# A token-and-channel mixing kernel behind random-feature attention: a new job order, new slots and new engines for the same operations

## The chip, the cores and the metric

The kernel runs on one core of a Trainium2 chip. The core has five engines with a queue each: PE (TensorE, matrix products), DVE (VectorE), ACT (ScalarE), POOL (GpSimd) and SP (which here only issues DMAs). PE writes its results to eight banks of PSUM; DVE and ACT read them from there and write to the on-chip memory SBUF. The metric is the device time of one execution in microseconds, the median of several runs; less is better.

## The reference

Eight batches, 8 heads, 576 positions, head size 64, 128 random features. Attention without softmax gives `x`; a mixing over the positions and one over the channels follow, each with a skip connection.

```
def phi(x):                       # q and k, scaled by 64 ** -0.25
    proj = einsum('bhsd,md->bhsm', x, omega)
    h = proj - sum(x * x) / 2
    return exp(h - max(h)) / sqrt(128)
kv  = einsum('bhsm,bhsd->bhmd', k_p, v);   z = sum_s k_p
x   = (q_p @ kv) / (q_p @ z + 1e-06)       # to (8, 576, 512)
u   = x + (relu(x^T @ w_tok1) @ w_tok2)^T  # 576 -> 256 -> 576
out = u + relu(u @ w_ch1) @ w_ch2          # 512 -> 1536 -> 512
```

## The kernel before

Each batch is worked as 512 main positions, in four blocks of 128, and 64 tail positions. The tails of two batches fill the 128 rows of a block, and those of all eight make a ninth "batch" for the channel mixing. So there are nine channel-mixing stages, 0 to 8; the text calls them stage 0 to 8.

The program is a list of 1211 jobs. Each job has an engine and a function that issues its instructions. The lists at the top of the file say everything about time: `ORDER` is the order in which the functions are called, and so the order of each engine's own queue; a negative number in it is a filler matmul on zeros, into the bank that it names. `SLOT` gives, in that order, the bank or ring slot that a job's new buffer takes. `MOVED` puts single jobs on another engine than the usual one. Within an engine nothing overtakes; between engines semaphores hold a job until its operands are there and its bank is free.

The jobs of one batch, by the names in the code, with their lines:

- `kp`, `qp`, `kt`, `qt` (L650 to L669): features of k and q; ACT takes their exponentials (L515).
- `km` (DVE, L681) the maximum of a key's features, `vs` (POOL, L687) the scaled v, `kv` (PE, L702), `kv_out` its copy, `num` (PE, L735), `num_out` (DVE, L744) the division, which gives `x`.
- `t1`, `t2` (PE, L778 and L791) the token mixing, with `t1_tail` (L771); its relu goes to ACT or DVE; `uadd` (DVE, L794) adds `x`. `htt` (PE, L845) is the same for the tails of two batches, with two adds on DVE (L851). Then a DMA transposes `u`; in batch 0 PE does that, with copies `ut_out`.
- `c1` (PE, L967), 12 jobs of four matmuls, each with a relu on ACT or DVE (L290, L292).
- The second product of the channel mixing. In stage 0 it is plain (`c2`, L1001). In stages 1 to 8 `channel_out_fast` (L858) does it in seven products in place of eight (L917, 12 matmuls each), with sums of the relu's blocks and differences of the weights. The products have the numbers k0 to k6. k0 and k1 read the relu's blocks as they are, and so does k6, behind the first sum; k2 reads the third sum, k3 the first, k4 the second and k5 the fourth. The four sums (L879) are made in two halves of 128 x 768, each half in a chain of four. A product is added to the output by a read on DVE (L906). Stage 8 does each product in two halves.

In the job lists, an ACT or DVE job that the planner may move asks `engine(...)` for its place. The sums do that too:

```
def tt(eng, **kw):
    (nc.gpsimd if eng == "POOL" else nc.vector).tensor_tensor(**kw)
...
    e_sum = engine("DVE")
    def go(...):
        o, a, b = what()
        tt(e_sum, out=o[:, part], in0=a[:, part], in1=b[:, part], op=op)
    job = add(e_sum, 0.5, key + KEYS["S"] + 0.1 * g + 0.01 * k, go, deps=[*need, *prev], take=[("S", c)])
```

Of the kernel before, what the change touches and what calls it, by code (L numbers as in the profile page):

```python
# [81 lines left out]
]  # L82
SLOT = (
    "0001203450670100531642027046313724005203716031213170242506371243501030126450300623741115037622415010"
    "3157143302010163207240531170360711422336140014632220751302761220105427113005401216030201704522131743"
    "5632010231741610520432015370243105072320714330625120712006304015123156124230220105611334112101502001"
# [985 lines left out]
```

## Time and profile before

| what | value |
|---|---|
| median of three runs | 283.71 us (283.15 to 284.58) |
| span of the profiled execution, from its first to its last instruction | 281.1 us |
| the profiled execution's own time | not listed beside its span; the runs above stand for it |
| PE busy | 270.3 us, 96% |
| DVE busy | 222.4 us, 79% |
| ACT busy | 138.6 us, 49% |
| POOL busy | 92.0 us, 33% |
| instructions | 6278 |

The page divides the span into 40 slices and writes the busy tenths of each engine. The table of stretches gives for any window each engine's busy microseconds and its count of instructions, then the granted PE clock, the busy share of the DMA engines and the GB/s. The chain of waits follows the work that ended last back through what released it. In the timeline a row has its start, its length, the engine, the line, what it writes and reads, its shape and the number of instructions merged into it; in brackets stands how long the engine was idle before and who ended that. The length of a matmul is modelled with its way through the array, so a row of several is a little longer than the number times the pitch.

### The profile page before, as it was taken

The page shows a single profiled execution, that of the slowest core. Times are in us where ns is not written, and L with a number is a line of the kernel's source. Part 1 is how long each engine was busy: PE and PEld are TensorE (multiplying, and loading weights), DVE is VectorE, ACT ScalarE, POOL GpSimd, SP SyncE. Part 2 cuts the span into 40 slices and gives each one's busy share as a digit, 9 for nine tenths or more (in the row PEclk, how much of TensorE's full clock was granted, in tenths as well). Part 3 has the DMA queues.
Part 4 walks back from the last instruction along what each step waited for, and adds up shares of the span by engine and source line. Part 5 has one row for each costly group of instructions (what it writes and reads, how often), then busy time and mean ns, then how long its engine had stood idle before and what let it go on. Part 6 is the DMA issues. An engine that isn't in the chain of part 4 may idle for free.

```text
span 281.1 us, 6278 instructions
## 1 busy us (share of the span) xinstructions
PE 270.3 (96%) x2526; PEld 167.6 (60%) x2526; DVE 222.4 (79%) x462; ACT 138.6 (49%) x288; POOL 92.0 (33%) x116
## 2 busy tenths in 40 slices
PE   6899999999999999999999999999999999999993
PEld 2547546443657755665667647755676467446782
DVE  2589828499999899996997999977995893565992
ACT  1498994049676418743758445734753510031200
POOL 8574994007510872048008710510033000000001
PEclk9999999999999999999999999999999999999999
DMA  6999999999998999997979993960151304030125
GB/s 161 194 189 161 157 169 213 178 191 202 179 218 184 148 172 186 181 198 104 212 178 185 241 135 101 161 156 2 76 97 59 111 0 96 0 149 2 75 90 135
DMA packets 80524, 39.66 MB, mean 141 GB/s; under 512 B 63984, under 2 KB 76016, under 8 KB 80304
## 3 DMA queue, kind: packets, MB, share of 16 engines
q0 software_dynamic: 31744, 17.74, 44.1%
q1 hardware_dynamic: 46832, 15.77, 29.1%
q10 hardware_dynamic: 1920, 5.77, 5.4%
q8 instruction: 19, 0.31, 0.4%
q14 instruction: 9, 0.07, 0.1%
HBM read 35.95 MB, written 16.52 MB: 187 GB/s over the span
## 4 chain that ended last, share of the span: by engine, by line
PE 89%; DVE 3%; DMA 2%; ACT 2%; issue 0%; SPq 0%; DVEq 0%
PE bank L967 32%; PE bank L917 26%; PE bank L791 5%; PE bank L778 5%; PE bank L1001 4%; PE bank L735 3%; PE bank L657 3%; PE bank L702 3%; DMA wc<-in_k_dram 2%; PE bank L669 2%; ACT kp L515 1%; PE bank L845 1%; PE bank L817 1%; PE bank L737 1%; PE bank L771 1%; DVE T L448 1%
## 5 line engine op out<-in xcount | busy, mean ns | idle before, releaser
L967 PE MATMUL bank<-uT,wc 128*128 128x512 f16 x376 | 89.6, 379 | 0.5 <-DVE r L292 0.4
L290 ACT ACTIVATE r<-bank 128x512 f16<-128x512 f32 (+1 forms) x86 | 47.7, 601 | 82.7 <-PE bank L967 61.5
L295 POOL TENSOR_TENSOR vs<-v,vs 128x512 f16<-128x512 f16 x32 | 34.2, 1072 | 94.4 <-DVE vs L683 51.3
L967 PEld LDWEIGHTS <-wc 128*128 128x128 f16 x424 | 38.8, 98 | 38.8 <-issue 1.6
L917 PEld LDWEIGHTS <-r 128*128 128x128 f16 x384 | 36.8, 98 | 8.2 <-issue 1.1
L515 ACT ACTIVATE kp<-bank 128x512 f16<-128x512 f32 x64 | 36.7, 618 | 8.9 <-PE bank L657 7.1
L515 ACT ACTIVATE qp<-bank 128x512 f16<-128x512 f32 x64 | 36.7, 614 | 8.8 <-PE bank L669 5.8
L681 DVE TENSOR_REDUCE km<-kp 128x8 f16<-128x1024 f16 x32 | 38.7, 1208 | 1.2 <-ACT kp L515 1.1
L292 DVE TENSOR_SCALAR r<-bank 128x512 f16<-128x512 f32 (+1 forms) x40 | 26.3, 670 | 15.7 <-PE bank L967 11.3
L745 DVE TENSOR_TENSOR x<-bank,rc 128x320 f16<-128x320 f32 x62 | 30.5, 492 | 2.1
L917 PEld LDWEIGHTS <-S 128*128 128x128 f16 x288 | 28.1, 98 | 5.8 <-issue 0.3
L906 DVE TENSOR_TENSOR o<-u,bank 128x512 f32<-128x512 f16 x28 | 19.0, 679 | 6.2 <-PE bank L917 5.8
L917 PE MATMUL bank<-T,r 128*128 128x256 f16 x192 | 23.8, 273 | 0.0
L917 PE MATMUL bank<-wc,r 128*128 128x256 f16 x192 | 23.6, 273 | 0.0
L917 PE MATMUL bank<-T,S 128*128 128x256 f16 x192 | 23.4, 273 | 0.0
L946 POOL DMA_DIRECT2D out_dram<-o x2 | 1.3, 645 | 61.2 <-issue 61.2
L906 DVE TENSOR_TENSOR o<-o,bank 128x512 f32<-128x512 f32 (+1 forms) x27 | 16.6, 617 | 2.5 <-PE bank L917 1.8
L735 PEld LDWEIGHTS <-qp 128*128 128x128 f16 x256 | 13.5, 98 | 8.1 <-DVE kvsb L286 0.7
L794 DVE TENSOR_TENSOR u<-x,bank 128x512 f16<-128x512 f16 x28 | 17.6, 680 | 0.0
L735 PE MATMUL bank<-kvsb,qp 128*128 128x65 f16 x256 | 15.0, 193 | 0.5 <-DVE kvsb L286 0.5
L791 PE MATMUL bank<-r,w 128*128 128x512 f16 x56 | 14.1, 381 | 0.0
L744 DVE RECIPROCAL rc<-bank 128x5 f32<-128x5 f32 x62 | 11.4, 184 | 2.9 <-PE bank L737 2.2
(119 smaller groups left out, 379.0 us busy)
## 6 DMA issues: line engine op xcount, KB each, us to landing
out_dram<-o ACTq DMA_DIRECT2D x9, 512.0 KB, 2.7
q<-in_q_dram POOLq DMA_DIRECT2D x6, 576.0 KB, 9.7
wc<-in_moe_w_ch_dram POOLq DMA_DIRECT2D x4, 768.0 KB, 9.0
k<-in_k_dram POOLq DMA_DIRECT2D x6, 512.0 KB, 7.8
v<-in_v_dram POOLq DMA_DIRECT2D x6, 512.0 KB, 9.9
out_dram<-o SPq DMA_DIRECT2D x5, 512.0 KB, 3.9
r<-in_q_dram POOLq DMA_DIRECT2D x4, 288.0 KB, 7.5
v<-in_v_dram POOLq DMA_DIRECT2D x4, 256.0 KB, 8.1
```

The costliest lines, as they stand in the source:

```text
L290: nc.scalar.activation(out=out, in_=in_, func=AF.Relu)
L292: nc.vector.tensor_relu(out=out, in_=in_)
L295: (nc.gpsimd if eng == "POOL" else nc.vector).tensor_tensor(**kw)
L515: nc.scalar.activation(out=out, in_=in_, func=AF.Exp, bias=0.0, scale=1.0)
L681: nc.vector.reduce_max(out=mx, in_=kpv, axis=AX.X)
L735: nc.tensor.matmul(ps[:, k, j * 65 : (j + 1) * 65], st, s[:, i, 0 : D + 1], start=True, stop=True)
L745: nc.vector.tensor_tensor(out=t_x[place("x", b)][:, :, (2 * hp + hs[0]) * D : (2 * hp + hs[0] + n) * D].rearrange("p j (i d) -> p i j d", ...
L791: nc.tensor.matmul(ps, w2_of(tb, j), r1[:, tb, :], start=(tb == 0), stop=(tb == NT - 1))
L794: nc.vector.tensor_tensor(out=t_u[place("u", b)][:, j, :], in0=t_x[place("x", b)][:, j, :], in1=bank(n), op=ALU.add)
L906: nc.vector.tensor_tensor(out=o, in0=a, in1=ps, op=ALU.add)
L917: nc.tensor.matmul(ps[:, j * DH : (j + 1) * DH], a[:, cb, j * P : (j + 1) * P], w[:, cb, :], start=(bank_of(b, j0) not in held and j == j0 ...
L967: nc.tensor.matmul(ps, wc1[:, db, cb * P : (cb + 1) * P], moving(db), start=(db == 0), stop=(db == ND - 1))
```

## The change

`ORDER`, `SLOT` and `MOVED` are new; nothing else is. The operations, their number and their shapes are the same: 1211 jobs and 23 fillers in both. 147 of the jobs change their label: 33 relus go from ACT to DVE and 26 the other way, 19 `kv_out` change sides, 6 `vs` and 2 `vbd` go from POOL to DVE, 38 sums are labelled "ACT" in place of "DVE", and the stores are spread anew over SP, ACT and POOL. Of the fillers, 18 stand ahead of PE's first transposes, where 8 stood.

The diff, cut to its core. The lines of the new `ORDER` are those of the head and of the parts of stages 2, 3, 4, 6 and 8 that the prediction walks through.

```diff
 ORDER = [
-    4, 3, 0, 2, 5, 7, 1, 6, 16, 14, 10, 15, 9, 8, 12, 38, 11, -1, -2, -3, -4, -5, -6, -7, -8, 39, 41, 13, 44,
-    42, 21, 40, 47, 45, 48, 76, 22, 46, 77, 67, 43, 68, -4, -6, 120, 18, 105, 78, 107, 82, -3, 49, 71, 106, 122,
...
+-1, -2, -1, -2, -1, -2, -1, -2, -1, -2, -1, 5, -2, -1, 4, -2, -1, -2, -1, 7, 0, 8, 1, 2, -2, 38, 39, 14, 16, 3, 41, 43, -2, 9, 10, 49, 51, 50, 47, 6,
+44, 71, 40, 90, 92, 91, -6, 42, 76, 77, 78, 48, 67, -1, 46, 120, 121, 122, 45, 105, 68, 106, 70, 96, 17, 23, 12, 52, 53, 54, 82, 79, -1, -5, 107, 111,
...
+644, 628, 630, 629, 416, 643, 423, 424, 439, 606, 440, 534, 535, 532, 533, 435, 614, 616, 656, 657, 658, 625, 627, 626, 443, 441, 444, 542, 536, 537,
+865, 618, 607, 660, 661, 662, 615, 436, 647, 648, 540, 541, 543, 538, 539, 445, 446, 437, 447, 448, 773, 737, 739, 774, 442, 775, 759, 738, 760, 761,
...
+566, 636, 550, 567, 557, 558, 568, 868, 458, 551, 552, 569, 570, 555, 556, 571, 572, 790, 791, 667, 787, 788, 670, 671, 575, 576, 577, 873, 875, 776,
+778, 578, 573, 777, 668, 669, 579, 870, 1001, 872, 871, 766, 676, 677, 580, 741, 780, 767, 674, 675, 768, 678, 679, 789, 574, 874, 792, 672, 673,
...
+1022, 1019, 814, 917, 839, 840, 819, 820, 825, 918, 826, 894, 829, 891, 823, 830, 904, 905, 906, 837, 838, 712, 723, 724, 907, 908, 892, 921, 922,
...
+962, 964, 952, 974, 1068, 1070, 969, 965, 966, 959, 960, 967, 968, 970, 979, 1071, 955, 1074, 1075, 1072, 956, 954, 975, 983, 976, 984, 1073, 1080,
+1078, 1081, 1082, 1083, 1079, 1085, 1086, 1138, 1076, 1077, 1084, 980, 864, 977, 981, 978, 987, 985, 988, 990, 989, 991, 992, 995, 996, 998, 1157,
...
+1163, 1164, 1173, 1175, 1171, 1174, 1172, 1177, 1178, 1176, 1199, 1200, 1167, 1168, 1169, 1165, 1166, 1181, 1182, 1170, 1184, 1179, 1180, 1188, 1189,
...
 MOVED = {
...
+"DVE", 300: "DVE", 304: "ACT", 308: "ACT", 337: "DVE", 350: "DVE", 362: "DVE", 376: "DVE", 378: "DVE", 392: "DVE", 418: "DVE", 420: "DVE", 424: "DVE",
+428: "DVE", 435: "ACT", 436: "ACT", 437: "ACT", 442: "ACT", 496: "DVE", 533: "DVE", 550: "DVE", 564: "DVE", 566: "DVE", 573: "ACT", 574: "ACT", 575:
+"ACT", 576: "ACT", 578: "ACT", 648: "DVE", 662: "DVE", 669: "DVE", 671: "DVE", 688: "DVE", 690: "DVE", 702: "DVE", 705: "ACT", 706: "ACT", 711: "ACT",
+712: "ACT", 727: "ACT", 754: "DVE", 805: "DVE", 822: "DVE", 824: "DVE", 830: "DVE", 832: "DVE", 834: "DVE", 838: "DVE", 841: "ACT", 842: "ACT", 843:
+"ACT", 844: "ACT", 846: "ACT", 847: "ACT", 848: "ACT", 863: "ACT", 864: "ACT", 930: "DVE", 958: "DVE", 960: "DVE", 962: "DVE", 968: "DVE", 974: "DVE",
+977: "ACT", 978: "ACT", 979: "ACT", 980: "ACT", 981: "ACT", 982: "ACT", 997: "ACT", 1038: "DVE", 1066: "DVE", 1075: "DVE", 1088: "DVE", 1094: "DVE",
+"DVE", 1165: "ACT", 1166: "ACT", 1167: "ACT", 1168: "ACT", 1169: "ACT", 1200: "SP", 1201: "ACT", 1203: "ACT", 1204: "SP", 1206: "SP", 1208: "SP",
```

What the numbers are:

| jobs | what |
|---|---|
| 41, 44; 49 | transposes of the two halves of batch 0's k; of half of its q |
| 435 to 442 | the eight sums of stage 2; 445 its k1, 446 that read, 447 its k2 |
| 571 to 578 | the sums of stage 3; 670, 668 `t1` of batch 4, 671, 669 their relus, 579 k0 of stage 3, 676 a `t2` |
| 712 | the last sum of stage 4; 837, 838 a `c1` of stage 5 and its relu; 723 k5 of stage 4 |
| 841 to 848 | the sums of stage 5 |
| 975 to 982 | the sums of stage 6; 983 k0, 984 its read, 987 k2, 985 k1; 1076 to 1083 the `t2` and `uadd` of batch 7, 1085 and 1086 the tail product and its two adds |
| 1163 to 1170 | the sums of stage 8; 1177 half of its k1, 1178 and 1176 reads of k1, 1181 half of its k2 |

More of the change, by code (lines that the diff above doesn't have):

```diff
@@ L22 @@
 ORDER = [
[59 rows of a table removed]
[42 rows of a table added]
 ]
 SLOT = (
-    "0001203450670100531642027046313724005203716031213170242506371243501030126450300623741115037622415010"
-    "3157143302010163207240531170360711422336140014632220751302761220105427113005401216030201704522131743"
-    "5632010231741610520432015370243105072320714330625120712006304015123156124230220105611334112101502001"
-    "1163320402165140211610176412517304000612037524002145223000117023104325137202120117305042100576141135"
-    "2740507154076110042751603114022705011041315732121403000112045010725110200405061403012301765403706427"
@@ L89 @@
-    "5643015206241073100625101246023220116534201330523111135160224716051246514725364700113516422103135174"
-    "1625317524300060120373642501100433627516043075122761076423700560420017305611117230017341570146002140"
-    "73521450047113602"
+    "00230450106730024151073206301241730201124067051272050243312061711504213136202431062050043071020400350210420061713717235423026027302351401531"
+    "02204104231405140160050312673421053215403700057004603132140531110262051121063710021051030516105607412303004302620110765063412406721033157100"
@@ L92 @@
+    "01272115314270115211211206705322005317150007253014711267456020220265314721000500143673312047062146642210750011204052052145311712121515001705"
+    "04735317107507220143307514601000106045001335234710200374252061212276020601510413612104506436464252633017101712120500633402322606120130400520"
+    "16435002322405210161207272645547050740217105336061112073117105123274003253072012123406140035751754507641317064571570613407210151363604761603"
+    "64100114041003311"
 )
 MOVED = {
-    42: "DVE", 43: "ACT", 45: "ACT", 48: "DVE", 51: "ACT", 53: "ACT", 56: "ACT", 60: "ACT", 62: "ACT", 65:
@@ L95 @@
-    "ACT", 75: "DVE", 129: "ACT", 137: "DVE", 139: "DVE", 141: "DVE", 145: "ACT", 147: "DVE", 163: "ACT", 169:
-    "DVE", 171: "ACT", 175: "DVE", 179: "ACT", 190: "ACT", 194: "ACT", 228: "ACT", 242: "DVE", 256: "DVE", 265:
-    "DVE", 278: "DVE", 280: "DVE", 286: "DVE", 300: "DVE", 324: "ACT", 399: "DVE", 426: "DVE", 428: "DVE", 432:
-    "DVE", 434: "DVE", 484: "DVE", 498: "DVE", 552: "DVE", 556: "DVE", 562: "DVE", 593: "ACT", 594: "ACT", 634:
-    "DVE", 662: "DVE", 690: "DVE", 692: "DVE", 700: "DVE", 702: "DVE", 727: "ACT", 768: "DVE", 796: "DVE", 822:
@@ L100 @@
-    "DVE", 828: "DVE", 830: "DVE", 836: "DVE", 838: "DVE", 863: "ACT", 904: "DVE", 970: "DVE", 997: "ACT", 998:
-    "ACT", 1024: "DVE", 1052: "DVE", 1088: "DVE", 1092: "DVE", 1094: "DVE", 1096: "DVE", 1098: "DVE", 1102:
-    "DVE", 1104: "DVE", 1108: "DVE", 1133: "ACT", 1134: "ACT", 1140: "DVE", 1148: "DVE", 1150: "DVE", 1152:
-    "DVE", 1160: "DVE", 1200: "SP", 1205: "ACT", 1206: "SP", 1207: "ACT", 1208: "SP",
+42: "DVE", 43: "ACT", 48: "DVE", 50: "ACT", 51: "ACT", 53: "ACT", 56: "ACT", 60: "ACT", 62: "ACT", 71: "DVE", 83: "DVE", 85: "ACT", 112: "DVE", 114:
@@ new lines @@
+"ACT", 129: "ACT", 135: "DVE", 137: "DVE", 145: "ACT", 149: "ACT", 152: "DVE", 157: "DVE", 159: "DVE", 161: "DVE", 171: "ACT", 173: "DVE", 179: "ACT",
+180: "ACT", 184: "ACT", 189: "ACT", 190: "ACT", 194: "ACT", 195: "ACT", 214: "ACT", 228: "ACT", 242: "DVE", 263: "DVE", 280: "DVE", 288: "DVE", 292:
+"DVE", 300: "DVE", 304: "ACT", 308: "ACT", 337: "DVE", 350: "DVE", 362: "DVE", 376: "DVE", 378: "DVE", 392: "DVE", 418: "DVE", 420: "DVE", 424: "DVE",
+428: "DVE", 435: "ACT", 436: "ACT", 437: "ACT", 442: "ACT", 496: "DVE", 533: "DVE", 550: "DVE", 564: "DVE", 566: "DVE", 573: "ACT", 574: "ACT", 575:
@@ L104 @@
+1096: "DVE", 1098: "DVE", 1102: "DVE", 1106: "DVE", 1110: "DVE", 1111: "ACT", 1114: "ACT", 1116: "ACT", 1117: "ACT", 1118: "ACT", 1152: "DVE", 1158:
+"DVE", 1165: "ACT", 1166: "ACT", 1167: "ACT", 1168: "ACT", 1169: "ACT", 1200: "SP", 1201: "ACT", 1203: "ACT", 1204: "SP", 1206: "SP", 1208: "SP",
+1210: "SP",
 }
```

89 rows, old and new, of the table ORDER are left out of this document.

## The prediction

> **What bounds the kernel now.** I read the page first: busy shares, slices, the chain.
>
> ```profile
> PE 270.3 (96%) x2526; PEld 167.6 (60%) x2526; DVE 222.4 (79%) x462; ACT 138.6 (49%) x288; POOL 92.0 (33%) x116
> ...
> PE   6899999999999999999999999999999999999993
> ...
> DVE  2589828499999899996997999977995893565992
> ACT  1498994049676418743758445734753510031200
> ...
> PE 89%; DVE 3%; DMA 2%; ACT 2%; issue 0%; SPq 0%; DVEq 0%
> ```
>
> TensorE (PE) is busy in every slice but the first, second and last, and 89% of the chain is PE. A new order cannot shorten PE's own work, which is the same list of matmuls. It can only take away idle time: in the head, between stages, and at the end. What there is to win is small; what there is to lose is every microsecond in which PE stands before an operand that VectorE (DVE) has not made. So the second view is the table by stretches of time.
>
> ```profile
> core 0: us, PE busy (x) PEld busy (x) DVE busy (x) ACT busy (x) POOL busy (x), PEclk, DMA share, GB/s
> 12.00:35.00 23.00, 21.85 (x347) 13.87 (x347) 20.22 (x43) 21.14 (x54) 16.99 (x22) 1.00 1.11 173
> 180.00:209.00 29.00, 29.00 (x274) 18.77 (x273) 25.00 (x53) 16.55 (x34) 4.35 (x5) 1.00 0.42 88
> ```
>
> From 12 to 35 us ScalarE (ACT) with 21.14 of 23.00 us and DVE with 20.22 carry the head. In a middle batch (180 to 209 us) PE is busy in all 29.00 us while DVE works 25.00 of them. So DVE has some 4 us of slack in 29: enough on average, but PE is kept free of waits only by where in DVE's queue each operation stands.
>
> **The prices.** Back-to-back pieces of the chain of waits (start, length) and of the timeline give the pitch of each operation.
>
> ```profile
> 44.68 0.86 PE bank L967 x4
> 265.73 10.52 PE bank L917 x96
> ```
>
> ```profile
> 171.01 2.47 DVE L794 TENSOR_TENSOR u<-x,bank 128x512 f16<-128x512 f16 x4
> 174.00 1.37 DVE L851 TENSOR_TENSOR ut<-x,bank 64x512 f16<-64x512 f16 x2
> ...
> 240.64 0.69 DVE L292 TENSOR_SCALAR r<-bank 128x512 f16<-128x512 f32 x1 [3.65 <-PE bank L967]
> 245.82 1.29 DVE L292 TENSOR_SCALAR r<-bank 128x512 f16<-128x512 f32 x2 [0.97 <-PE bank L967]
> 266.45 0.56 DVE L295 TENSOR_TENSOR S<-r 128x768 f16<-128x768 f16 x1 [0.39 <-ACT r L290]
> 269.72 1.02 DVE L295 TENSOR_TENSOR S<-r,S 128x768 f16<-128x768 f16 x2
> 271.32 0.41 DVE L906 TENSOR_TENSOR o<-ut,bank 128x256 f32<-128x256 f16 x1
> ```
>
> On PE a 512-column matmul is 0.86 / 4 = 0.22 us, so a `t1` or `c1` job 0.86 and a `t2` job 0.43; an output product (12 of the 96) is 10.52 / 8 = 1.31, a half one of the last stage 0.66. On DVE a relu is 0.60 (1.29 - 0.69), a sum of `channel_out_fast` 1.02 - 0.56 = 0.46, a `uadd` 0.60 (2.47 less 0.68, by three), a half read up to 0.41, the pair's tail add 1.37. A whole read moves as many columns as a `uadd`: 0.60.
>
> **What the change does to the sums.** `MOVED` now names "ACT" for 38 of the 64 sums. But a sum is issued by `tt`, which knows POOL and otherwise takes `nc.vector`: the sums stay on DVE, whatever the label. 38 x 0.46 = 17.5 us of DVE work that the new lists place as ACT's therefore still stand in DVE's queue, at the places where the lists put them, with what DVE has to do behind them. I walked each stage by hand, from the job order and the prices above. Stage n is the channel mixing of batch n, stage 8 that of the tails; k0 to k6 are its seven output products.
>
> Stage 6. When product k0 (983) ends, PE has four `t2` (1.73) and the pair's tail product 1085 (0.43 if its half-width matmuls run side by side, 0.86 if not) and then stands before k2 (987), which needs sums 977 and 981. PE is there after 2.2 to 2.6 us. DVE in that time: the read 984 (0.60), four `uadd` (2.40), the tail add (1.37), and only then sums 980, 977, 981 (1.38): 5.75 us. PE stands 3.2 to 3.6 us; I take 3.4. Product k1, which could have filled 1.31 of it, is behind k2.
>
> Stage 8. After the half product 1177 nothing is left for PE before k2 (1181). DVE has two half reads (0.82) and sums 1167, 1168, 1169, 1165 (1.84): 2.6 us.
>
> Stage 2. After k1 (445) DVE has the read 446 (0.60) and sum 437 (0.46) before k2 (447) may start: 1.06; the three `uadd` and `kv_out` ahead, with sum 436 among them, leave it up to 0.45 later. 1.3.
>
> Stage 4. Sum 712 stands behind relu 838, whose `c1` (837) is PE's job just before k5 (723): 0.60 + 0.46, 1.1 us.
>
> Stage 3. Five sums (2.30) stand between relus 671 and 669: DVE is through 3.50 us after product 670. PE has `t1` 668 and k0 (2.17) and two small jobs, some 0.5 together: 0.8 us before `t2` 676.
>
> In stages 1, 5 and 7 the moved sums cost nothing: in 5, 841 to 848 (2.30) are hidden by two `t1` and k0 (3.03). Without that cover they would cost what 3 does. Sum: 3.4 + 2.6 + 1.3 + 1.1 + 0.8 = 9.2 us; with the ends above and 0.2 of latency to each hand-over, 8 to 11.
>
> That the old order does not stand like this is seen in the rows of its stage 5.
>
> ```profile
> 199.23 1.02 DVE L295 TENSOR_TENSOR S<-r,S 128x768 f16<-128x768 f16 x2
> 200.17 2.48 DVE L794 TENSOR_TENSOR u<-x,bank 128x512 f16<-128x512 f16 x4
> 200.75 1.47 PE L917 MATMUL bank<-T,S 128*128 128x256 f16 x12
> ```
>
> There the last two sums run ahead of the four `uadd`, and k2 (T,S) starts at 200.75, before the `uadd` are through. Stage 6 of the new order has these two groups the other way round.
>
> **The head.** It is changed wholly: 18 filler matmuls instead of 8 before the first transposes, the loads of q and v in another order, `q` transposes (49) ahead of the second half of `k` (44).
>
> ```profile
> 1.19 3.60 PE L1039 MATMUL bank<-S 128*128 128x512 f16 x8 [1.19 <-DVE S L1036]
> 9.10 1.12 PE L470 MATMUL bank<-S,wc 64*128 64x64 f32 x15 [1.27 <-DMA wc<-in_k_dram]
> 11.28 1.04 PE L1039 MATMUL bank<-S 128*128 128x512 f16 x2
> 15.98 1.89 PE L1039 MATMUL bank<-S 128*128 128x512 f16 x8
> ...
> 1.20:5.00 3.80, 3.59 (x8) 1.03 (x8) 0.79 (x10) 1.28 (x1) 3.64 (x7) 1.00 0.75 176
> ```
>
> ```profile
> 2.22 0.59 POOL L319 DMA_DIRECT2D r<-in_q_dram  x1
> 2.78 1.42 POOL L351 DMA_DIRECT2D vt<-in_v_dram  x2
> ...
> 10.80 0.60 ACT L515 ACTIVATE kp<-bank 128x512 f16<-128x512 f32 x1
> 13.32 1.57 ACT L515 ACTIVATE kp<-bank 128x512 f16<-128x512 f32 x3 [0.95 <-PE bank L657]
> ...
> r<-in_q_dram POOLq DMA_DIRECT2D x4, 288.0 KB, 7.5
> ```
>
> The first q load goes behind the two `vt` loads: issued at 2.2 + 1.4 = 3.6, with 7.5 to land 11.1 us, or 9.7 if it lands as before. PE's job 44, at 9.10 now, waits behind 49 for it: 0.6 to 2 us late, and ACT's first exponential goes from 10.80 to about 12. Against that ACT does two of its copies before, and 0.8 us more of PE's work stands ahead of the first `c1` (counted in the two lists). Four evictions (two `kv_out`, two `ut_out`) come to ACT here, two `vs` and one `vbd` to DVE. I find the two heads equal to within my arithmetic: +0.5 us, ends -2 and +3. A `vs` on DVE has no row; between one sum of the same kind (0.46) and POOL's own time for it.
>
> ```profile
> L295 POOL TENSOR_TENSOR vs<-v,vs 128x512 f16<-128x512 f16 x32 | 34.2, 1072 | 94.4 <-DVE vs L683 51.3
> ```
>
> Six of them, 0.46 to 1.07 each: 3 to 6 us on DVE over the whole span, with slack around them by the table of stretches; taken at nothing, 1 us at the upper end.
>
> One rule is to be weighed here. The first eight fillers take 3.60 / 8 = 0.45 us, those at 15.98 only 0.24, though PEclk in the table of stretches is 1.00 for both (1.20 to 5.00 and 12 to 35 us): the pitch shows the slow clock, the column does not. The Trainium skill, "TensorE: Matmul & The Clock Gate", Part 1, says that PE runs at half clock until it has been busy for a window of about 3.4 us, and falls back after an idle one. By that rule the new head is at full clock before its first transpose, and the estimate for the head would be -1 us instead of +0.5.
>
> **The end.** The last stores are spread anew: SP issues nine of twelve, ACT two, POOL one.
>
> ```profile
> 272.11 5.64 SPq L946 DMA_DIRECT2D out_dram<-o  x6
> 276.27 0.42 DVE L906 TENSOR_TENSOR o<-o,bank 128x256 f32<-128x256 f32 x1 [0.23 <-PE bank L917]
> ```
>
> SP now spends up to 5.64 / 6 = 0.94 on one, waits included. Five of them fall into the last two half products: +0.5 us (0 to 1.5).
>
> **Sum.** 9.2 + 0.5 + 0.5 = 10.2 us on the span of 281.1: 291.3. Around the span lie 2.6 us (median 283.7 less 281.1; the profiled execution has no other time listed), so 293.9 us.
>
> **Rivals.** Faster: the longer run of fillers takes the slow clock out of the head. The head can give 2 us, hence 281.7. It decides only if the sums cost under 2 us in all, which needs DVE some 3 us ahead of PE at stages 6 and 8; against it, the reads 984 and 1178 cannot start before PE's own products end. The place is visible: two fillers at 11.28 take 1.04 us, half pitch still, and ACT's kp at 13.32 stood 0.95 us for PE. 8 in 100. Partly hidden: only stages 6 and 8 stand (6.0), the head gives 1.5 and the end nothing: 283.7 + 4.5 = 288; 12 in 100. Worse: the late q and v hold the head by 3 us, DVE's late `uadd` delay the `uT` transposes of one or two batches by 2 us: 293.9 + 4.5 = 298; 13 in 100. Clock: PE might come out of the long stand of stage 6 at the slow pitch of the first fillers (0.45 us against 0.24) and keep it as long as those eight did, 3.60 us; that would cost up to 3.2 us more, 297; 4 in 100, since no row shows a warm PE idle for so long. By the Trainium skill, "TensorE: Matmul & The Clock Gate", Part 1, an idle window of about 3.4 us brings the half clock back, a length that this stand only just reaches. That the label of the sums does what it says would be the first rival again, since `tt` cannot put them on ACT.
>
> **Numbers.** The forecast itself has 63 in 100 (290 to 297). A measurement of this kernel tells 0.5% (1.4 us) from no change. Faster 0.08 is the first rival; the same 0.03 is the edge between it and the second; slower 0.89 all else. The range leaves out the first rival and the upper half of the worse ones: 286.5 to 299.
>
> **What would show it.** In the profile after: no sum on ACT, DVE with 64 of them; PE waiting for DVE's S at L917 before k2, once for about 3.4 us near 230 to 240 us and once for 2.5 near the end; stages 5 and 7 without such a wait; the first `kp` exponential near 12 us; PE's busy time unchanged while the span grows. I am wrong if these two waits are under 1 us, or if the stretch up to the first `c1` moved by over 3 us.

## The result, and the profile after

| | kernel before | kernel after |
|---|---|---|
| median | 283.45 us | 338.77 us |
| lowest to highest | 283.15 to 284.58 | 336.18 to 344.55 |
| profiled execution: span; its own time | 281.1 us | 336.0 us; 338.19 us |
| ratio after / before | | 1.191, interval 1.186 to 1.196 |

The kernel after is 19% slower. Forecast were 293.9 us (286.5 to 299). (283.45 us is the median of four runs; the 283.71 above was of three.) Some executions of every kernel fall in a slower state of the chip; the ratios are formed without them, the medians with them, so the two can differ. Of the page, the rows that answer to those shown of before:

```profile
PE 282.8 (84%) x2526; PEld 170.7 (51%) x2526; DVE 232.6 (69%) x469; ACT 138.1 (41%) x289; POOL 83.9 (25%) x107
...
PE   7789996954920999997898999998999978999963
...
PEclk9969998995985699999999999999999997999998
...
PE 49%; DMA 27%; DVE 16%; POOL 2%; issue 2%; ACT 1%; DVEq 0%; POOLq 0%
```

PE's share of the chain fell from 89 to 49%; 27% are now transfers (2% before), 16% are VectorE (3% before). There is a hole in the 12th and 13th of the 40 slices (92 to 109 us), and the granted clock falls in several slices. In the kernel before, that row was:

```profile
PEclk9999999999999999999999999999999999999999
```

PE's idle time grew from 281.1 - 270.3 = 10.8 to 336.0 - 282.8 = 53.2 us, its busy time by 12.5 us for the same matmuls. What PE waited for (the view of waits: total, times, longest):

```profile
PE bank L535 <- DMA kT<-k: 15.4, 1, 15.4
PE bank L950 <- DMA uT<-u: 8.8, 1, 8.8
PE bank L900 <- DVE S L278: 8.4, 4, 3.2
PE bank L640 <- DMA kT<-k: 3.1, 1, 3.1
...
PE bank L774 <- DVE r L275: 1.3, 1, 1.3
```

(Lines are 17 lower than in the kernel before: L900 is its L917.) The third and the fifth row are the forecast term, 9.7 us. The other three, 27.3 us, are waits for DMA transposes, which the prediction did not have. The transposes are issued by SP; its timeline (start, time to issue) in the kernel after, and below it in the kernel before:

```profile
38.09 8.36 SPq L363 DMA_TRANSPOSE kT<-k  x1
46.62 10.13 SPq L363 DMA_TRANSPOSE qT<-q  x1
60.74 7.79 SPq L782 DMA_TRANSPOSE uT<-u  x1
68.63 15.91 SPq L363 DMA_TRANSPOSE qT<-q  x1
84.72 10.05 SPq L363 DMA_TRANSPOSE kT<-k  x1
```

```profile
53.71 2.71 SPq L380 DMA_TRANSPOSE kT<-k  x1
56.47 4.03 SPq L380 DMA_TRANSPOSE qT<-q  x1
60.55 1.85 SPq L799 DMA_TRANSPOSE uT<-u  x1
```

What took 2 to 4 us now takes 8 to 16, and SP issues one after the other: `kT` of batch 3 starts at 84.72 because `qT` holds SP until 84.54. (The chain of waits below puts PE's L950 ahead of it; but between 84.54 and 84.72 SP's own rows leave no room for a wait.) It lands at 110 us:

```profile
60.74 19.78 DMA uT<-u
80.57 4.15 PE bank L950 x11
84.72 25.24 DMA kT<-k
```

In the table of stretches the whole core stands there, with its DMA engines busy, and PE comes out of such a stand at a low clock (the column behind POOL):

```profile
95.00:110.00 15.00, 0.00 (x0) 0.00 (x0) 0.00 (x0) 0.00 (x0) 0.00 (x0) 0.59 1.36 123
...
56.15:58.50 2.35, 2.35 (x28) 1.32 (x29) 0.25 (x1) 1.85 (x4) 0.61 (x1) 0.59 1.57 156
58.50:61.00 2.50, 2.39 (x8) 0.72 (x6) 2.10 (x4) 1.19 (x3) 0.77 (x2) 0.70 2.26 219
80.57:82.50 1.93, 1.93 (x5) 0.72 (x6) 0.00 (x0) 0.00 (x0) 0.83 (x2) 0.50 1.75 137
82.50:85.00 2.50, 2.50 (x9) 0.94 (x8) 0.00 (x0) 0.87 (x2) 0.90 (x2) 0.72 1.46 94
110.00:112.50 2.50, 2.50 (x18) 1.16 (x19) 1.31 (x4) 1.63 (x4) 0.10 (x1) 0.50 1.48 59
112.50:115.00 2.50, 2.50 (x8) 0.92 (x7) 2.32 (x2) 0.20 (x1) 2.20 (x3) 0.58 1.28 34
```

PE's busy time there times what is missing of the clock (PE busy 2.35 at 0.59 loses 2.35 x 0.41) is 1.7 + 1.7 + 2.3 = 5.7 us lost behind the three stands. So the span's 54.9 us are: 27.3 waits for transposes, 5.7 slow matmuls behind them, 9.7 waits for sums and the relu behind sums, 1.6 slow matmuls behind the longest of these (stage 6, below), 3.1 in the head's slow clock (20.56 us busy at 0.85, below), together 47.4. The other 7.5 I did not follow singly; small stands in the head and behind it are among them (1.0 in stage 2, 0.7 in stage 5).

What goes on in the DMA engines is in the view of DMA for a stretch: packets, megabytes and share by queue. POOL's loads are the software queue, SP's transposes q1. First the kernel after from 84 to 110 us, then the kernel before from 56 to 64:

```profile
q1 hardware_dynamic: 4836, 1.22, 70.0%
q0 software_dynamic: 4577, 2.01, 67.8%
```

```profile
q1 hardware_dynamic: 5939, 1.50, 114.7%
```

Before, in these 8 us no load runs, and the transposes move 1.50 MB. After, loads run beside them, and they move less, 1.22 MB, in 26 us. In shorter pieces of it the packets come out nearly one for one at first: 1056 of the loads to 1060 of the transposes from 84 to 88 us, 199 to 192 from 98 to 101, where the loads' are larger and take 0.53 MB to 0.05. From 101 to 110 us the count is uneven, 333 to 1423, and the transposes still move only 0.36 MB in 9 us. Taking turns by packet does not account for that last piece. Among the packets of the loads from 98 to 110 us are 25 of 18 KB, each 1.4 us long, all of them casts of q or k; the trace does not tell which of the 16 engines a packet ran on, so whether the transposes wait behind these is not shown.

### The profile page after: what moved, and what is told of

It reads as the page before. It is cut to its first block, busy times and chain, and to the rows that moved or that the text cites. A ratio compares the mean times of both kernels' runs of the same rounds, so it can differ in the third digit from the quotient of the medians.

```text
span 336.0 us, 6254 instructions
## 1 busy us (share of the span) xinstructions
PE 282.8 (84%) x2526; PEld 170.7 (51%) x2526; DVE 232.6 (69%) x469; ACT 138.1 (41%) x289; POOL 83.9 (25%) x107
## 4 chain that ended last, share of the span: by engine, by line
PE 49%; DMA 27%; DVE 16%; POOL 2%; issue 2%; ACT 1%; DVEq 0%; POOLq 0%
PE bank L950 22%; PE bank L900 17%; DMA kT<-k 13%; DMA uT<-u 6%; DMA r<-in_q_dram 5%; DMA q<-in_q_dram 4%; DVE S L278 3%; DVE o L889 2%; DVE km L664 2%; PE bank L774 2%; DVE u L777 2%; PE bank L761 2%; DVE r L275 1%; PE bank L718 1%; PE bank L685 1%
## 5 line engine op out<-in xcount | busy, mean ns | idle before, releaser
L950 PE MATMUL bank<-uT,wc 128*128 128x512 f16 x376 | 91.4, 390 | 9.0 <-DMA uT<-u 8.8
L273 ACT ACTIVATE r<-bank 128x512 f16<-128x512 f32 (+1 forms) x79 | 44.1, 593 | 99.8 <-PE bank L950 92.2
L950 PEld LDWEIGHTS <-wc 128*128 128x128 f16 x424 | 40.1, 100 | 54.6 <-DMA uT<-u 9.0
L278 POOL TENSOR_TENSOR vs<-v,vs 128x512 f16<-128x512 f16 x26 | 28.5, 1098 | 99.6 <-DVE vs L666 76.5
L900 PEld LDWEIGHTS <-r 128*128 128x128 f16 x384 | 37.0, 98 | 8.5 <-issue 2.1
L275 DVE TENSOR_SCALAR r<-bank 128x512 f16<-128x512 f32 (+1 forms) x47 | 30.9, 676 | 14.0 <-PE bank L950 11.2
L498 ACT ACTIVATE kp<-bank 128x512 f16<-128x512 f32 x64 | 35.1, 624 | 8.3 <-PE bank L640 8.3
L900 PEld LDWEIGHTS <-S 128*128 128x128 f16 x288 | 27.7, 100 | 15.9 <-DVE S L278 10.1
L900 PE MATMUL bank<-T,S 128*128 128x256 f16 x192 | 24.7, 282 | 8.4 <-DVE S L278 7.5
L900 PE MATMUL bank<-wc,r 128*128 128x256 f16 x192 | 23.8, 275 | 1.0 <-DVE u L777 0.7
L900 PE MATMUL bank<-T,r 128*128 128x256 f16 x192 | 23.6, 273 | 0.0
L774 PE MATMUL bank<-r,w 128*128 128x512 f16 x56 | 15.6, 407 | 1.7 <-DVE r L275 1.3
L574 DVE TENSOR_REDUCE kmt<-kpt 128x4 f16<-128x512 f16 x7 | 4.7, 672 | 17.1 <-ACT kpt L498 17.1
L718 PE MATMUL bank<-kvsb,qp 128*128 128x65 f16 x256 | 16.1, 196 | 0.2 <-DVE x L728 0.2
```

The costliest lines, as they stand in the source:

```text
L273: nc.scalar.activation(out=out, in_=in_, func=AF.Relu)
L275: nc.vector.tensor_relu(out=out, in_=in_)
L498: nc.scalar.activation(out=out, in_=in_, func=AF.Exp, bias=0.0, scale=1.0)
L718: nc.tensor.matmul(ps[:, k, j * 65 : (j + 1) * 65], st, s[:, i, 0 : D + 1], start=True, stop=True)
L774: nc.tensor.matmul(ps, w2_of(tb, j), r1[:, tb, :], start=(tb == 0), stop=(tb == NT - 1))
L900: nc.tensor.matmul(ps[:, j * DH : (j + 1) * DH], a[:, cb, j * P : (j + 1) * P], w[:, cb, :], start=(bank_of(b, j0) not in held and j == j0 ...
```

## The experiments

My theory A: the new order of POOL's queue sets loads of later batches in flight early, and these share the DMA engines with the transposes on which PE waits. Rival B: SP's own new order holds the transposes. Ratios are to the kernel before, on the same chip.

| run | median, us | ratio, interval |
|---|---|---|
| e1_loads | 349.01 | 1.233, 1.227 to 1.239 |
| e2_sums | 331.75 | 1.157, 1.149 to 1.166 |
| e12_both | 341.12 | 1.205, 1.198 to 1.212 |
| e3_mirror | 307.04 | 1.070, 1.064 to 1.076 |
| e5_nocast | 310.80 | 1.091, 1.088 to 1.095 |
| e10_loads2 | 331.27 | 1.160, 1.153 to 1.166 |
| e13_keep3 | 314.50 | 1.109, 1.101 to 1.117 |
| e9_nocast_sums | 301.49 | 1.062, 1.057 to 1.067 |
| e8_stage6 | 289.78 | 1.020, 1.017 to 1.023 |
| e8_fill | 287.25 | 1.012, 1.008 to 1.016 |
| e6_fill | 283.11 | 0.995, 0.993 to 0.997 |
| e12_fill2 | 283.30 | 0.997, 0.994 to 1.000 |

**The old places of the loads.** POOL's queue from the first half of `wc2` (25) on; 212 to 254, 348, 390, 471, 510 and 524 are its `vs` and `vbd` jobs of batches 1 to 3, the rest are loads:

```diff
-25, 327, ..., 226, 460, 254, 596, 330, 459, 464, 465, 597, 461, 866, 595, 729, 348, 466, 600, 390, 1000, 601, 731, 602, 999, 471, ...
+25, 460, 327, ..., 332, 459, 226, 254, 330, 348, 390, 461, 465, 464, 466, 597, 595, 471, 510, 596, 524, 600, ...
```

> The kernel after, with POOL's loads of batches 3 to 7 put back to the places that they had in POOL's old queue; every other queue as in the kernel after. Theory A (the early loads share the 16 DMA engines with SP's transposes of kT and uT, PE waits for these, and then runs at a slow clock): the three waits of 15.4, 8.9 and 3.1 us go to under 5 in all, and some 10 us of slow matmuls go with them: 338.8 - 27.4 + 4 - 10 = 305 us (299 to 312). Theory B (the transposes are late because of their own order on SP, which stays): 336 to 341, no change. Theory C (what counts is the load order of the head and of batch 2, which stays): the wait of 3.1 stays, the others halve, 318 to 326.

It became slower, 349 us: none of the three. PE's waits (first fence) and POOL's timeline (second) say why:

```profile
PE bank L555 <- DMA kT<-k: 17.4, 2, 10.2
PE bank L794 <- DVE u L797: 10.0, 1, 10.0
```

```profile
74.12 1.05 POOL L298 TENSOR_TENSOR vs<-v,vs 128x512 f16<-128x512 f16 x1 [10.40 <-DVE vs L686]
75.11 0.57 POOL L367 DMA_DIRECT2D k<-in_k_dram  x1
```

The cast of batch 3's `k`, ahead of `vs` job 348 in the kernel after, now stands behind 348 and 390 and is issued at 75.11 instead of 60.78 us. PE's new order needs its `kT` no later than before, and waits again. The 10.0 us for `u` come the same way round: a store that SP issues at 151.92, behind a `kT` whose issue took 5.44 us, lands at 158.75, and DVE's next read waits for it with the `uadd` behind it. So the early loads are not a plain mistake of the new order; it needs some of them early. The same edit together with the sums' (below):

> Both edits together, the loads and the sums. Theory A with the sums: 305 - 10 = 295 us (289 to 302), the two effects add. Theory B: as the sums alone, 325 to 331. If loads and sums hide each other, more than 3 us above the sum of the two single effects.

341.1 us, 8 less than the loads' edit alone and outside what A and B said: the sums' part adds, the loads' part is as wrong as by itself.

**The same loads in the old order of PE.**

POOL's queue of the kernel before, from the same place on:

```diff
-25, 460, 29, 33, 326, ..., 327, 332, 337, 459, 390, 461, 465, 362, 464, 376, 348, 466, 597, 595, 510, 596, ...
+25, 29, 326, 327, 325, 33, ..., 332, 460, 596, 330, 459, 464, 465, 597, 461, 866, 595, 729, 337, 390, 362, 376, 348, 466, ...
```

> The kernel before, with POOL's loads of batches 2 to 7 in the order of the kernel after (tails of batches 3, 4 and 6, and the q and k of batches 4 and 5, ahead of loads that batch 2 and 3 need), merged into POOL's old queue; two tail loads of v stand later, since their buffers aren't free before. PE's, DVE's, ACT's and SP's queues as in the kernel before. Theory A: transposes of kT and uT late here too, PE stands 15 to 30 us in all: 300 to 320 us. Theory B: 282 to 287.

1.070 times the kernel before, some 20 us more, with all other queues untouched. The profiled execution took 309.96 us, the quickest of the four 302.17. In it PE waits for `uT`, as in the kernel after, and for `wc2` on top, whose second half (33) stands later here:

```profile
PE bank L965 <- DMA uT<-u: 13.9, 2, 11.9
PE bank L999 <- DMA wc<-in_moe_w_ch_dram: 6.6, 1, 6.6
```

So the load order by itself makes a late `uT`. B falls for this part: SP's order is that of before.

**Without the casts.** In `load_transposed`:

```diff
-            scratch[w, b] = tc.dram_tile([H * RA, 2 * D], FP16, name=f"{w}16_{b}")
+            scratch[w, b] = tc.dram_tile([H * RA, 2 * D], FP16, name=f"{w}16_{b}") if b == NPE else scratch[w, NPE]
...
             def cast(w=w):        # and in cast_main, cast_tail
+                if b > NPE:
+                    return
```

> The kernel after, without the loads that cast q and k of batches 3 to 7 to 16 bits (some 5.8 of the 17.6 MB of the software queue); these batches work on the q and k of batch 2, so that part of the computation is left out. All queues keep their order, and SP issues the same transposes. Theory A (the loads in flight take turns with the transposes in the DMA engines): a transpose takes 3 to 6 us again, PE's waits of 15.4 and 8.9 us for kT and uT go to under 3 in all, the 3.1 us for the first kT stay, and some 6 us of slow matmuls go: 338.8 - 22 - 6 = 311 us (303 to 317). Theory B (the order on SP itself holds the transposes): the two waits stay, 333 to 340.

310.8 us, as by A. But batch 3's own casts are gone here as well. The next kernel keeps them:

```diff
-            scratch[w, b] = tc.dram_tile([H * RA, 2 * D], FP16, name=f"{w}16_{b}")
+            scratch[w, b] = tc.dram_tile([H * RA, 2 * D], FP16, name=f"{w}16_{b}") if b <= NPE + 1 else scratch[w, NPE + 1]
...
+                if b > NPE + 1:
+                    return
```

> The kernel after, without the casts of q and k of batches 4 to 7 only (these work on batch 3's, that part of the computation is left out); batch 3's own casts stay where the kernel after has them. If the loads of the later batches, queued ahead of their need, are what slows the transposes of batches 2 and 3 and of u: the waits of 15.4 and 8.9 us shrink to under 5 in all, 312 to 318 us. If batch 3's own casts land too late: the wait for its kT stays over 8 us, 322 to 335.

314.5 us. Of the waits for transposes this is left, and SP issues `qT` and `kT` of batch 3 (second fence) in 5.8 and 2.8 us where the kernel after took 15.9 and 10.1:

```profile
PE bank L646 <- DMA kT<-k: 3.7, 1, 3.7
PE bank L608 <- DMA qT<-q: 1.4, 1, 1.4
```

```profile
66.37 5.79 SPq L369 DMA_TRANSPOSE qT<-q  x1
72.39 2.84 SPq L369 DMA_TRANSPOSE kT<-k  x1
```

The order on SP and the casts of batch 3 are those of the kernel after; of the loads issued up to these waits only such are gone as nobody needs yet. That decides for A against B: the loads, not SP's order.

**The loads in the order of the batches.** POOL's queue of the kernel after:

```diff
-226, 460, 254, 596, 330, 459, 464, 465, 597, 461, 866, 595, 729, 348, 466, 600, 390, 1000, 601, 731, 602, 999, 471, ...
+226, 254, 330, 460, 459, 461, 464, 465, 466, 348, 596, 597, 595, 600, 390, 601, 602, 471, 735, 734, 510, 730, 731, 729, ...
```

> The kernel after, with POOL's loads in the order of the batches: those of batch 3 early as in the kernel after, those of batch 4 only behind the first vs of batch 2, those of batch 5 behind vbd of batch 3, and so on; all other queues as in the kernel after. Theory A, with what the first load experiment showed (loads that come back to their old place stand behind vs jobs, and PE waits for kT of batches 3 and 4 all the same): the transposes around 60 to 95 us run with little beside them, PE's waits for kT and uT go from 27.4 to under 10 us in all: 310 to 322 us. Theory D (the new order of PE asks for kT of batches 3 and 4 earlier than any order of loads can bring it): the sum of these waits stays over 20 us, 330 to 350.

331.3 us is in the range of D, the waits lie between A and D: 4.4 for `kT` of batch 2, 8.8 for `qT`, 1.0 for `uT`; 14.2 of the 27.3 us are left. A better order of the loads brings half of these waits back, but only 7.5 us of the median, since PE now stands 3.4 us for a `u` and 2.5 for a relu (0.4 and 1.3 in the kernel after). Whether any order brings the rest is open.

**Transfers alone.** A kernel of its own; the transposes stand on SP's queue, the loads on POOL's:

```
def pair():
    for t in tT:
        nc.sync.dma_start_transpose(out=t.unsqueeze(1), in_=scratch)
...
    for i in range(4):
        wc(i)          # nc.gpsimd.dma_start, 128 x 4 rows of w_ch1
    pair()
```

> No mixing at all, only transfers: a pair of the kernel's DMA transposes (2304 x 128, 16 bits) alone, then with loads from POOL beside it: rows of v (1 KB), blocks of w_ch1 (3 KB rows), casts of q (9 KB rows, DRAM to DRAM), casts of tails (64 numbers a row), then alone again. Theory A: alone some 3 us of issue each and 6 us to landing (2.7 to 4 and 6.0 to 6.8 in the kernel before); beside the 3 and 9 KB rows two to four times that, since each packet of 256 B waits its turn behind a long one; beside the short rows less than twice. Theory B: the same 6 to 7 us to landing in every case, within a factor of 1.3.

The view of DMA, first for 54 to 58 us (transposes alone), then for 65 to 81 (beside `w_ch1`):

```profile
q1 hardware_dynamic: 3966, 1.00, 114.2%
```

```profile
q0 software_dynamic: 1830, 2.74, 93.8%
q1 hardware_dynamic: 1830, 0.46, 22.1%
...
kT<-k SPq DMA_TRANSPOSE x2, 14.7
```

1830 packets of each queue in 16 us: one for one. Loads of 1.5 KB a packet leave the transposes of 256 B 0.46 MB in 16 us, against 1.00 MB in 4 us alone, a ninth of the rate. The quickest transpose alone took 4.3 us to landing; beside rows of `v` (512 B a packet) the slowest took 16.0, beside `w_ch1` 22.2, five times as long where two to four were expected. (The 14.7 above is the median of this one and a later one of 7.2.) The phases ran into each other: POOL issued the casts of q and of the tails at the start, beside the first pair. From 6.8 to 12 us 92 packets of the casts moved 1.12 MB, and 31 of the first transpose 0.01 MB; it landed after 16.7 us. From 20 to 24 us, beside the tail casts, the count is uneven, 3445 packets with 0.10 MB to 1968 with 0.50 MB.

**The sums.** DVE's queue, stage 6 (likewise in stages 2, 3, 4 and 8):

```diff
-975, 976, 984, 1081, 1083, 1079, 1086, 1077, 980, 977, 981, 978, 988
+975, 976, 980, 977, 981, 978, 984, 1081, 1083, 1079, 1086, 1077, 988
```

> The kernel after, with sums moved ahead in DVE's queue at five places (stage 2: 436, 437 ahead of the uadds; stage 3: relu 669 ahead of three sums; stage 4: 712 ahead of relu 830; stage 6: 980, 977, 981, 978 ahead of read 984; stage 8: all six sums that k2 needs ahead of read 1130). Nothing else moved. By the prediction's step the stands of PE before k2 and t2 (1.4, 1.3, 1.0, 3.2, 2.9: 9.7 us) go, with some 1.5 us of slow matmuls behind the longest: 338.8 - 11 = 328 us (325 to 331). If these stands only take up slack that a later wait gives back, 334 to 339.

By the ratios (1.191 - 1.157) x 283.4 = 9.6 us gone, give or take some 3, less by the medians (7.0). No wait of PE at that line for S is left over 0.3 us.

The same edit in the kernel without casts:

> The kernel after with both causes taken out: no casts of q and k for batches 3 to 7 (these work on batch 2's, that part of the computation is left out), and the sums ahead in DVE's queue as in the second experiment. If the two causes are the whole but for the head and the first kT (2.5 + 3.1 + 1.9 of slow matmuls, and some 4 in small stands): 310.8 - 11.4 - 4 = 295 us (292 to 298). If the sums are hidden by something else once the casts are gone: 300 to 308.

301.5, 9.3 us under the run without casts (8.3 by the ratios) but 6.5 above what I expected: where PE no longer stands for sums it stands for 1.8 us for a read, 2.5 for `uadd`, 1.6 for the tail add. My 4 us for "small stands" were too few.

**The sums of stage 6 in the old kernel, and the clock.**

DVE's queue of the kernel before, and then the job order at k2:

```diff
-975, 976, 979, 980, 981, 982, 977, 984, 978, 1077, 1079, 1083, 1086, 988, 1081
+975, 976, 979, 984, 1077, 1079, 1083, 1081, 1086, 980, 977, 981, 978, 982, 988
```

> The kernel before, with one place of DVE's queue as in the kernel after: in stage 6 the sums 980, 977, 981 and 978 stand behind the four uadds and the pair's tail add instead of ahead of them. Nothing else moved. By the prediction's step PE stands 3.2 to 3.6 us before k2 (987), then runs a short time at a slow clock (1.3 to 2.6 us lost, by the kernel after and by the run without casts): 283.7 + 3.4 + 1.9 = 289.0 us (287 to 290). If the stand is taken up by slack later in stage 7 or in the end: 284 to 285.5. If the clock does not fall after a single stand in a long busy stretch: 287.0.

```diff
-987, 989, 988, ...
+-6, -6, -6, -6, -6, -6, -6, -6, -6, -6, -6, -6, 987, 989, 988, ...
```

> The same kernel with twelve filler matmuls on zeros (2.6 us at full pitch) in PE's queue right ahead of k2, in a bank that is free. They fill the stand and cannot shorten it. If the slow clock after the stand is what costs beyond the stand itself, it stays at full speed here: 1.3 to 2.6 us faster than the same kernel without the fillers, 286.5 to 287.5. If the slow pitch comes from elsewhere: no gain, or the 12 fillers overrun the stand, +0 to +1.

289.8 and 287.3 us. PE's timeline of the first, then of the second:

```profile
234.10 4.45 PE L915 MATMUL bank<-T,S 128*128 128x256 f16 x24 [3.39 <-DVE S L293]
```

```profile
231.34 2.75 PE L1037 MATMUL bank<-S 128*128 128x512 f16 x12
234.89 2.93 PE L915 MATMUL bank<-T,S 128*128 128x256 f16 x24 [0.80 <-DVE S L293]
```

One place of DVE's queue costs 3.39 us of standing and 4.45 - 2.93 = 1.5 us of slow matmuls behind it, 4.9 of the 5.6 us by which this kernel's median is over that of the kernel before on the same chip (284.21). Fillers do not shorten the stand, but keep the clock: behind it 0.50 is granted without them and 1.00 with them.

**The fillers of the head.** In `ORDER` of the kernel before:

```diff
-..., -7, -8, 39, 41, 13, 44, ...
+..., -7, -8, -1, -2, -1, -2, -1, -2, -1, -2, -1, -2, 39, 41, 13, 44, ...
```

> The kernel before, with ten more filler matmuls behind its first eight, as the one part of the new head that needs no load: PE is busy longer before its first transposes. If the half pitch of the head's first matmuls (two fillers at 11.28 us took 1.04 us) is what holds the head: 283.4 - 1 to -2 = 281.5 to 282.5. If the loads of k and ACT's exponentials hold it: 283.4, within 0.5 us.

Half a per cent faster than the kernel before (0.993 to 0.997); in its trace the first `c1` starts 0.6 us earlier (32.90 for 33.54), of which 0.2 are left at the first `c2`. That is less than the 1.7 us between the medians (283.11 and, for the kernel before on this chip, 284.78); the rest I cannot place.

With that, in POOL's queue:

```diff
-25, 460, 29, 33, 326, 32, ...
+25, 29, 33, 326, 460, 32, ...
```

> The kernel before with the ten extra fillers of the earlier run, and with the tail casts of batches 2 and 3 (326, 460) behind the second half of wc2 (33) in POOL's queue: in the run with fillers alone PE's gain of 0.65 us in the head shrank to 0.2 at the first c2, which waits for wc2. If that load bounds c2: 0.4 us more than the fillers alone, 0.7% under the kernel before; if not, the 0.5% of the fillers alone; if the tail casts now come late for kT of batch 2: slower by 1 us or more.

0.997, an interval that overlaps that of the fillers alone: no gain on top is shown. In its trace the first `c2` starts earlier, at 46.49 for 47.34 us, and waits 0.65 us for `wc2` (0.30 with the fillers alone), yet the span is the same, 281.0 for 280.9. So `wc2` still holds the first `c2`, and where the gain goes behind it is open.

## Why the prediction was wrong

**The sums were right.** Predicted were 3.4 us in stage 6, 2.6 in stage 8, 1.3 in 2, 1.1 in 4, 0.8 in 3, none in 1, 5 and 7, together 9.2. Measured are 3.2, 2.8, 1.4, 1.0 and 1.3, together 9.7, and none over 0.3 us in 1, 5 and 7 for a sum. DVE's timeline of stage 6 is the walk of the prediction line by line: the read, the `uadd` and the tail add, and only then the sums; PE's row below shows the wait.

```profile
273.05 0.69 DVE L889 TENSOR_TENSOR o<-u,bank 128x512 f32<-128x512 f16 x1 [0.42 <-PE bank L900]
273.66 1.97 DVE L777 TENSOR_TENSOR u<-x,bank 128x512 f16<-128x512 f16 x3
275.55 1.38 DVE L834 TENSOR_TENSOR ut<-x,bank 64x512 f16<-64x512 f16 x2
276.96 0.69 DVE L777 TENSOR_TENSOR u<-x,bank 128x512 f16<-128x512 f16 x1
277.56 0.55 DVE L278 TENSOR_TENSOR r<-r 128x768 f16<-128x768 f16 x1
278.03 1.02 DVE L278 TENSOR_TENSOR S<-S,r 128x768 f16<-128x768 f16 x2
...
278.64 2.74 PE L900 MATMUL bank<-T,S 128*128 128x256 f16 x12 [3.22 <-DVE S L278]
```

**The clock rival happened, smaller.** It had 4 in 100 and up to 3.2 us. The prediction held PE's busy time unchanged; it grew by 12.5 us, of which the slow clock makes 1.6 here, 5.7 behind the transposes and 3.1 in the head. The k2 above takes 2.74 where the prediction's row had 1.47; with the stretch behind it 2.66 x 0.50 + 2.70 x 0.11 = 1.6 us are lost. The stand in the old kernel shows it by itself.

```profile
278.64:281.30 2.66, 2.66 (x13) 1.87 (x14) 0.88 (x2) 0.00 (x0) 0.00 (x0) 0.50 0.81 157
281.30:284.00 2.70, 2.70 (x24) 2.29 (x23) 0.69 (x1) 0.00 (x0) 0.00 (x0) 0.89 0.27 50
```

**The head** was given +0.5, ends -2 and +3. The first exponential comes at 11.93 us, "about 12" as predicted; the first `c1` at 36.03 instead of 33.54, +2.5, inside the ends but not at the value. The rest of the head runs slower than its work:

```profile
12.00:35.00 23.00, 20.56 (x310) 13.84 (x309) 20.55 (x42) 22.62 (x60) 16.91 (x23) 0.85 1.26 200
```

**The end** was given +0.5: from PE's last matmul to the end of the span it is 5.4 us, 4.9 before.

**The step that failed** is a term that was missing. The prediction priced the moved loads only in the head, and there only those that came late; transposes got 2 us, inside the rival called "worse", and only through late `uadd`. No term stood for loads that come earlier on POOL's queue, and what they do to SP's transposes: 27.3 us of waits and 5.7 of slow matmuls, 33 of the 45 us that the forecast was short. With the casts of batches 3 to 7 left out the time is 310.8 us, with batch 3's kept 314.5. The lists would have given a warning. Ahead of `vs` job 348 the old order has casts 459, 461 and 460 of batch 3; the new one adds 595, 597, 596 of batch 4, 729 of batch 5 and 866 of batch 6. With 576 KB for a cast of q, 512 for one of k and 64 for two tails (the page's DMA issues) that is 2.9 MB in place of 1.2. In the kernel after POOL issues them between 38.72 and 64.82 us, and SP its first four transposes between 38.09 and 68.63.

The Trainium skill, "DMA: Bandwidth & Descriptors", section "Queues, rings and completion order", says that each DMA engine goes round the queues that have work, a packet at a time. The trace agrees beside `w_ch1`: 1830 packets to 1830; beside the tail casts it does not, 3445 to 1968. (The page's packet is a group of descriptors, the profile's a single record.) By that rule a transpose of small packets gets, beside a load, as many packets as the load and so a small part of the bytes; weighed in the prediction, it would have been the rival to name.

The label of the sums did what was read in `tt`: none of the 64 is on ACT, and DVE has them all.

## What to carry to other kernels

When a change moves loads ahead, count the bytes that are then in flight beside the transfers on the critical path, above all beside transposes with their small packets: where the queues took turns packet by packet here, the large packets won. An order of jobs is one thing over all queues: the early loads could not simply be put back, since the new order of PE needed some of them, and moving back all of them made it worse. And a stand of PE of 3 us or more cost more than its length in most cases here; fillers ahead of a wait that cannot be avoided kept the clock here.

## What the runs showed of the hardware

Beside loads of `w_ch1` the packets of the two DMA queues came one for one (1830 to 1830), and a transpose of 256-byte packets fell to a ninth of its rate beside packets of 1.5 KB. Beside casts of 18 KB a packet it all but stood (0.01 MB in 5.2 us). Beside the tail casts' packets, some 30 bytes each on average, the count was not even (3445 to 1968).

SP's issue of a transpose is not a fixed cost: 1.3 to 4.0 us in the kernel before, up to 18.5 us in the kernel after, beside loads. SP was held for that time, and what stood behind it in its queue came late too (the `kT` at 84.72).

The granted clock after a stand of PE: behind 3.1, 3.2, 3.4, 8.8 and 15.4 us the stretches read 0.5 to 0.6. In finer stretches of the kernel after it is 0.50 from 56.59 to 60.01, 77.07 to 83.90, 97.55 to 114.62 and 278.46 to 281.87 us, and 1.00 between these: 1, 2, 5 and 1 times 3.41 us. It begins as late as 0.4 us behind the end of a stand (56.15). Behind the stand of 2.8 us in stage 8, the same in the five traces whose sums stayed in place, the clock stayed at 1.00 in the kernel after and fell to 0.50 to 0.57 in the four others (`e1_loads`, `e5_nocast`, `e10_loads2`, `e13_keep3`); the kernel after and the last of these:

```profile
323.90:326.50 2.60, 2.60 (x24) 2.34 (x25) 1.84 (x4) 0.00 (x0) 0.00 (x0) 1.00 0.22 52
```

```profile
297.91:300.50 2.59, 2.59 (x13) 1.84 (x14) 1.42 (x3) 0.00 (x0) 0.00 (x0) 0.50 0.22 52
```

The Trainium skill, "TensorE: Matmul & The Clock Gate", Part 1, gives about 3.4 us as the idle window and calls it free-running. That one and the same stand of 2.8 us fell on both sides, and that the slow stretches are multiples of 3.41 us wherever PE's stands lie, agrees with the second; that 2.8 us were enough at all is less than the first would let one expect.
